# End of routing: gathers for nine chunks, hi and lo rows for the last two, two remainders on another engine

## The chip, the cores and the metric

The kernel runs on one core of a Trainium2 chip. The metric is the device time of one execution in microseconds. Before the change the median of three runs is 744.73 us (744.6 to 744.79). The time contains everything from the first load to the last write of the output.

## The reference

Retention, then a mixture of experts with capacity, then a dense mixture of four experts. Cut to what matters:

```python
# retention, B=2, H=8, S=768, head 64, x = y as (N=1536, D=512)
state = gamma * state + k_t (outer) v_t;  y_t = scale * q_t @ state
# first mixture: E=8, F=1024, capacity cap = N // E * 2 = 384
logits = x @ w_gate;  expert = argmax(logits);  gate = softmax(logits)[expert]
for i in range(N):            # in token order
    e = expert[i]
    if counts[e] < cap: disp[e, counts[e]] = x[i]; pos[i] = counts[e]; counts[e] += 1
y = relu(disp @ w1) @ w2;     out[i] = gate[i] * y[expert[i], pos[i]]
# second mixture: 4 experts on every token, weighted with normalised domain_probs
out += p[:, e] * (relu(x @ w1[e]) @ w2[e])
```

What the part below turns on: each token needs its expert, its rank among the tokens of that expert, and the rows of an expert must stand together before its matmuls can start.

## The kernel before

The 1536 tokens are 12 chunks of 128 (NT = 12). A first stage goes chunk by chunk through retention and routing, a second runs the eight experts of the first mixture on 224 slots each, a third the second mixture. Products in the second and third stage are three fp32r passes over high and low halves; `split_w` makes these halves for a block of weights: ScalarE casts the loaded block into the high half (line 124), and VectorE subtracts that from the block for the low half, the remainder (line 125).

The order of the work is written by hand: each engine runs its instructions in the order in which the program issues them. In the first stage, step `it` of the loop issues for chunk it-1 the state products, the state update, the second half of the output and its scaling (`st_I`, `st_U`, `st_O`, `st_x`), for chunk `it` the scores and their mask (`st_S`), for chunk it-2 the transposition with the gate logits (`x_pe`; `x_reduce` adds up the logits on VectorE, copies the rows to SBUF on ScalarE and writes them to `xd` in DRAM) and the argmax (`x_dve`), and for chunk it-3 the rank (`r_pe`, `r_dve`) with a slot matrix `at`, which says which token stands in which slot; `g_pe` turns it into indices in `slot_ps`. PSUM banks without a name of their own go round in fours, so that a tile needs the bank of the tile four before it.

Expert 0 is prepared apart, because it is needed first. For the chunks below NE = NT - 2 = 10, the indices of its slots are cast into `gidx0`, and GpSimd fetches its rows from `xd` with two indirect DMAs into `xe0`; `fetched` turns them with products against the identity into `xt0`. The rows of the last two chunks are added to `xt0` straight from SBUF: `r_dve` makes a one-hot matrix `at0` (which token of the chunk is in which slot of expert 0), and `late` multiplies the chunk's rows by it, as fp32.

At the end of routing the order is: state products of chunk 11, transposition of chunk 10, second half of chunk 11, index and gathers, transposition of chunk 11, one-hot products of chunk 10, of chunk 11, then the products on the gathered rows. `split_w(0)` stands in step 8 of the loop, `split_w(1)` behind all products. Then every engine reads a flag (line 580) and branches on it (line 581), ScalarE and VectorE split `xt0` into high and low halves (lines 713 and 717), and the matmuls of expert 0 begin (lines 860 and 863).

Weight blocks are loaded by SP into four buffers (`load_w`, line 111); a block's buffer is free when both its halves are made.

The lines quoted in words here are those of the profile:

Of the kernel before, what the change touches and what calls it, by code (L numbers as in the profile page):

```python
# [9 lines left out]
F32 = mybir.dt.float32  # L10
F32R = mybir.dt.float32r
F16 = mybir.dt.float16
I32 = mybir.dt.int32
AF = mybir.ActivationFunctionType
ALU = mybir.AluOpType
# [5 lines left out]
P = 128  # L21
B, H, S, HD = 2, 8, 768, 64
N, D, F = 1536, 512, 1024
E1, E2 = 8, 4
NCH = S // P
NT = N // P
NE = NT - 2
KD = D // P
KF = F // P
XW = KD * 136  # L30
# [25 lines left out]
def tile_retention_moe_moe(ctx: ExitStack, tc, qkv, cst, gqt, a1, a2, b1, b2, out, cap):  # L56
# [54 lines left out]
            nc.sync.dma_start(out=raws[u], in_=wsrc(u))  # L111
            nload[0] += 1

    def split_w(n):
        if n >= len(units) or units[n] in ws:
            return
        u = units[n]
        kind = u if isinstance(u, int) else u[0]
        if kind == "t":
            r = ts.pop(u[1])  # L120
        else:
            r = raws.pop(u)
        w = pw.tile([P, 2, 1024], F32R, tag="w", name=f"w{n}")
        nc.scalar.copy(w[:, 0], r)  # L124
        nc.vector.tensor_tensor(out=w[:, 1], in0=r, in1=w[:, 0].bitcast(F32), op=ALU.subtract)  # L125
        ws[u] = w
        if kind != "t":
            load_w(place[u] + 5)
# [47 lines left out]
    with ExitStack() as actx:  # L176
# [104 lines left out]
        def st_I(i):  # L281
            c = i % NCH
            live[i]["o"] = [bank(f"O{i}_{j}") for j in range(2)]
            q = live[i].pop("q")
            if c > 0:
                for hp in range(4):
                    for j in range(2):
                        r = slice(64 * j, 64 * j + 64)
                        nc.tensor.matmul(
                            out=o_at(i, hp, j), lhsT=st[c % 2][r, hp],  # L290
                            rhs=q[r, hp * P:(hp + 1) * P], start=(hp < 2), stop=False,
                            skip_group_check=True,
                        )
# [105 lines left out]
        def r_dve(i):  # L399
            rp = rl.pop(i)  # L400
            sel = p2.tile([P, 8], F32, tag="sel", name=f"sel{i}")
            rk = ranks[:, i:i + 1]
            yield nc.vector.tensor_tensor_reduce(
                out=sel, in0=rp, in1=ohs[:, i], scale=1.0, scalar=0.0, op0=ALU.mult, op1=ALU.add,
                accum_out=rk,
            )
            if i < NE:
                yield slot_at(i)
            else:
                at0[i] = p2.tile([P, SM], F32, tag="at0", name=f"at0_{i}")  # L410
                yield nc.vector.tensor_scalar(
                    out=at0[i], in0=rnk[:, 0:SM], scalar1=rk, scalar2=oh0.pop(i), op0=ALU.is_equal,
                    op1=ALU.mult,
                )

        def slot_at(i):
            at = ats[i] = p2.tile([P, SL], F16, tag="at", name=f"at{i}")
            return nc.vector.tensor_scalar(
                out=at, in0=rnk, scalar1=ranks[:, i:i + 1], scalar2=None, op0=ALU.is_equal
            )  # L420
# [16 lines left out]
        for it in range(NT):  # L437
# [27 lines left out]
                r_pe(it - 3)  # L465
                seqs.append(r_dve(it - 3))
            braid(*seqs)
            if it == 8:
                split_w(0)

        st_I(NT - 1)
        x_pe(NT - 2)
        r_pe(NT - 3)
        st_O(NT - 1)
        braid(r_dve(NT - 3))
        g_pe(NT - 4)
        g_pe(NT - 3)
        st_x(NT - 1)
        nc.vector.tensor_copy(gidx0, slot_ps[:, :, 0])
        xe0 = pq.tile([P, SL // P, D], F32, tag="kv", name="xe0")  # L480
        for b in range(SL // P):
            nc.gpsimd.indirect_dma_start(
                out=xe0[:, b], out_offset=None, in_=xd[0:1 + NE * P],
                in_offset=bass.IndirectOffsetOnAxis(ap=gidx0[:, b:b + 1], axis=0),
            )
        braid(x_dve(NT - 2))
        x_pe(NT - 1, False)
        r_pe(NT - 2)
        braid(r_dve(NT - 2))
        x_reduce(NT - 1)  # L490
        braid(x_dve(NT - 1))
        xt0 = [
            bank(f"T0x{g}", f"x{g}")[:, 0:2 * SM].rearrange("p (k t) -> p k t", k=2)
            for g in range(2)
        ]

        def late(i, ks=range(KD)):
            for k in ks:
                nc.tensor.matmul(
                    out=xt0[k // 2][:, k % 2], lhsT=xks[i][:, k * P:(k + 1) * P], rhs=at0[i],  # L500
                    start=(i == NE and k % 2 == 0), stop=True, skip_group_check=True,
                )

        def fetched(b, ks):
            w = min(SM - b * P, P)
# [4 lines left out]
                    start=False, stop=True, skip_group_check=True,  # L510
                )

        late(NE, range(KD - 1))
        r_pe(NT - 1)
        cps = bank("cnt")[:, 0:8]
        nc.tensor.matmul(out=cps, lhsT=onesb, rhs=cum[:, NT], start=True, stop=True)
        late(NE, range(KD - 1, KD))
        braid(r_dve(NT - 1))
        slot_at(NT - 2)
        slot_at(NT - 1)  # L520
        late(NE + 1)
        g_pe(NT - 2)
        g_pe(NT - 1)
        for ks in (range(2), range(2, KD)):
            fetched(0, ks)
            fetched(1, ks)
        nc.vector.tensor_scalar(
            out=cnt[:, 0], in0=cps, scalar1=float(cap), scalar2=None, op0=ALU.min
        )
# [1 line left out]
        if general:  # L531
# [7 lines left out]
                )  # L539
            nc.vector.tensor_copy(nbi[:, 0:8], nbf)  # L540
            nc.vector.tensor_reduce(out=nbi[:, 8:9], in_=nbf, axis=AX.X, op=ALU.max)
        split_w(1)
        nc.vector.tensor_copy(gidx, slot_ps)

    def offsets():
# [759 lines left out]
```

## Time and profile before

| | |
|---|---|
| median of three runs | 744.73 us |
| the profiled execution | 744.18 us |
| its span, first to last instruction | 742.4 us |
| TensorE busy | 727.5 us (98%) |
| VectorE, ScalarE, GpSimd busy | 469.0, 338.8, 167.6 us |
| first matmul of expert 0 | 68.13 us from the start of the span |
| mean granted TensorE clock | 0.997 |

A time in a row is microseconds from the span's start, the number behind it how long the piece took. A merged row of TensorE counts its pieces (x16); matmuls overlap, so a row's length is from its first start to its last end. An fp32 product shows as two instructions, an fp32r one as one. In brackets stands how long the engine was idle ahead of the row, and what ended that.

### The profile page before, as it was taken

Reading aid. Unit: us, or ns where it says so; the run is one execution under the profiler, and the core shown is the slowest. Engines: PE = TensorE matmul, PEld = TensorE weight load, DVE = VectorE, ACT = ScalarE, POOL = GpSimd, SP = SyncE. Lnnn points to the kernel's source line nnn. Section 1 sums busy time; section 2 is a strip of 40 time slices with the busy share of each in tenths; the row PEclk is TensorE's granted clock in tenths of the full one; section 3 lists DMA queues with packets and bytes.
Section 4 is the critical chain, followed back from the end, with each engine's and each line's share of the span. In section 5 each row is a group of like instructions: output and inputs, shape, how many; then the busy total and the mean of one; then the engine's idle time right before and its main releaser. Section 6 shows DMA issues by size and latency. Waiting matters only on the chain.

```text
span 742.4 us, 11359 instructions
## 1 busy us (share of the span) xinstructions
PE 727.5 (98%) x4466; PEld 661.8 (89%) x4467; DVE 469.0 (63%) x769; ACT 338.8 (46%) x545; POOL 167.6 (23%) x158
## 2 busy tenths in 40 slices
PE   8998999999999999999999999999999999999996
PEld 5887999999998888899988999889998899988895
DVE  4888889887887935634754645773375454557334
ACT  2334666675665624334443335633445334453341
POOL 3543111222310011222222211213421121111103
PEclk9999999999999999999999999999999999999998
DMA  9985876687561122211113122112221212112002
GB/s 336 409 325 160 298 259 217 214 277 240 201 200 57 40 75 64 103 61 57 57 60 100 41 85 86 58 62 95 100 72 72 86 56 86 58 57 86 29 0 86
DMA packets 27642, 93.22 MB, mean 126 GB/s; under 512 B 3617, under 2 KB 3889, under 8 KB 27586
## 3 DMA queue, kind: packets, MB, share of 16 engines
q1 hardware_dynamic: 23042, 81.79, 31.9%
q0 software_dynamic: 2672, 7.44, 3.2%
q10 hardware_dynamic: 1872, 3.24, 1.1%
q8 instruction: 36, 0.59, 0.3%
q14 instruction: 20, 0.16, 0.1%
HBM read 86.11 MB, written 6.34 MB: 125 GB/s over the span
## 4 chain that ended last, share of the span: by engine, by line
PE 85%; DVE 5%; DMA 5%; ACT 1%; issue 1%; POOL 1%; POOLq 0%; SPq 0%; ACTq 0%; DVEq 0%
PE o L1111 35%; PE a L955 17%; PE m L860 11%; PE b L955 8%; PE m L863 5%; PE bb L955 5%; DMA kv<-qkv 2%; DVE w L125 2%; DMA qk<-qkv 1%; DMA xd<-xk 1%; DVE tsum L889 1%; PE O L301 1%; PE S L246 1%; DMA raw<-a 1%; PE T L701 1%
## 5 line engine op out<-in xcount | busy, mean ns | idle before, releaser
L1111 PE MATMUL o<-w,g_c 128*128 128x512 f32 x1152 | 267.4, 390 | 0.0
L1111 PEld LDWEIGHTS o<-w,g_c 128*128 128x128 f32 x1152 | 215.8, 188 | 43.8
L125 DVE TENSOR_TENSOR w<-raw,w 128x1024 fp32r<-128x1024 f32 x128 | 158.2, 1245 | 16.9 <-ACT w L124 16.7
L955 PE MATMUL a<-X,w 128*128 128x384 f32 x720 | 145.1, 336 | 0.0
L124 ACT CAST w<-raw 128x1024 fp32r<-128x1024 f32 x128 | 132.6, 1048 | 5.9 <-DMA raw<-a 4.2
L990 DVE TENSOR_TENSOR c<-b,c 128x384 f32<-128x384 f32 x30 | 16.7, 558 | 181.2 <-PE b L955 181.2
L955 PEld LDWEIGHTS a<-X,w 128*128 128x128 f32 x720 | 127.3, 188 | 2.6 <-DVE c L990 0.3
L139 POOL TENSOR_TENSOR t<-raw 128x512 f32<-128x512 f32 x28 | 38.8, 1386 | 375.2 <-DMA raw<-b 326.9
L986 ACT COPY c<-a 128x384 f32<-128x384 f32 x60 | 28.7, 479 | 196.4 <-PE a L955 196.4
L860 PE MATMUL m<-h,w 128*128 128x448 f32 x256 | 81.7, 378 | 1.7 <-DVE h L890 1.7
L860 PE MATMUL m<-xet,w 128*128 128x448 f32 x256 | 80.8, 375 | 0.9 <-DVE xet L717 0.9
L971 ACT ACTIVATE g_c<-c 128x384 fp32r<-128x384 f32 x96 | 50.4, 526 | 66.2 <-DVE c L990 64.9
L955 PE MATMUL b<-X,w 128*128 128x384 f32 x360 | 72.0, 334 | 0.0
L863 PE MATMUL m<-h,w 128*128 128x224 f32 x256 | 67.4, 263 | 0.0
L863 PE MATMUL m<-xet,w 128*128 128x224 f32 x256 | 67.4, 263 | 0.0
L955 PEld LDWEIGHTS b<-X,w 128*128 128x128 f32 x360 | 63.5, 188 | 0.0
L975 DVE SCALAR_TENSOR_TENSOR g_c<-c,g_c 128x384 fp32r<-128x384 f32 x96 | 52.9, 552 | 4.0
L860 PEld LDWEIGHTS m<-h,w 128*128 128x128 f32 x256 | 48.0, 187 | 6.1 <-ACT w L124 2.2
L860 PEld LDWEIGHTS m<-xet,w 128*128 128x128 f32 x256 | 48.0, 187 | 4.7 <-PEq L581 1.0
L863 PEld LDWEIGHTS m<-h,w 128*128 128x128 f32 x256 | 48.8, 191 | 0.0
L863 PEld LDWEIGHTS m<-xet,w 128*128 128x128 f32 x256 | 48.8, 190 | 0.0
L955 PE MATMUL bb<-X,w 128*128 128x384 f32 x204 | 41.3, 339 | 0.1
(148 smaller groups left out, 747.1 us busy)
## 6 DMA issues: line engine op xcount, KB each, us to landing
raw<-a SPq DMA_DIRECT2D x64, 512.0 KB, 4.3
raw<-b SPq DMA_DIRECT2D x64, 512.0 KB, 3.5
qk<-qkv SPq DMA_DIRECT2D x12, 512.0 KB, 8.4
kv<-qkv SPq DMA_DIRECT2D x12, 512.0 KB, 8.3
xd<-xk ACTq DMA_DIRECT2D x12, 256.0 KB, 6.6
gqs<-gqt SPq DMA_DIRECT2D x6, 256.0 KB, 7.7
iw<-cst SPq DMA_DIRECT2D x1, 272.0 KB
xe<-xd,gidx POOLq DMA_INDIRECT x16, 4.2
```

What stands on the lines that cost most here:

```text
L124: nc.scalar.copy(w[:, 0], r)
L125: nc.vector.tensor_tensor(out=w[:, 1], in0=r, in1=w[:, 0].bitcast(F32), op=ALU.subtract)
L139: eng.tensor_tensor(out=c[:, 0:2], in0=b[:, 2:4], in1=b[:, 1:3], op=sub)
L246: nc.tensor.matmul(out=bks[j][:, cols], lhsT=qk[r, 1, cols], rhs=qk[r, 0, cols], start=True, stop=True,)
L860: nc.tensor.matmul(out=b2, lhsT=w[0], rhs=x, start=first, stop=last, skip_group_check=True)
L863: nc.tensor.matmul(out=b2[:, 0], lhsT=w[1], rhs=x[:, 0], start=False, stop=last, skip_group_check=True)
L955: nc.tensor.matmul(out=bk[:, 0:HT], lhsT=w[:, sw, k], rhs=x[:, sx, k], start=(first and m == 0), stop=(m == len(steps) - 1), skip_group_ch ...
L971: nc.scalar.activation(out=h2[:, 0], in_=src, func=AF.Relu)
L975: nc.vector.scalar_tensor_tensor(out=h2[:, 1], in0=src, scalar=0.0, in1=h2[:, 0].bitcast(F32), op0=ALU.max, op1=ALU.subtract,)
L986: nc.scalar.copy(t, bk[:, 0:HT])
L990: nc.vector.tensor_tensor(out=t, in0=bk[:, 0:HT], in1=t, op=ALU.add)
L1111: nc.tensor.matmul(out=bk, lhsT=h2[:, sh, cols], rhs=w[:, sw, k], start=(q == 0 and m == 0 and (n, t) not in begun), stop=(m == 2), skip_g ...
```

## The change

Four things move at the end of routing; what is computed stays the same.

- NE becomes NT - 3 = 9: the gathers cover nine chunks, and chunk 9 is added with one-hot products too, in fp32 as before.
- For chunks 10 and 11 the one-hot products are fp32r: `x_parts` casts the rows on ScalarE and takes the low rows on GpSimd, and `late` multiplies both by the one-hot matrix, high rows first.
- The output of chunk 11 is finished ahead of the transposition of chunk 10, and index and gathers come right after it. The products on gathered rows stand between those of chunk 10 and those of chunk 11.
- `split_w(0)` and `split_w(1)` go into steps 10 and 11 of the loop, with the subtraction on GpSimd.

```diff
-NE = NT - 2
+NE = NT - 3
-    def split_w(n):
+    def split_w(n, eng=nc.vector):
...
         nc.scalar.copy(w[:, 0], r)
-        nc.vector.tensor_tensor(out=w[:, 1], in0=r, in1=w[:, 0].bitcast(F32), op=ALU.subtract)
+        eng.tensor_tensor(out=w[:, 1], in0=r, in1=w[:, 0].bitcast(F32), op=ALU.subtract)
...
-                at0[i] = p2.tile([P, SM], F32, tag="at0", name=f"at0_{i}")
+                at0[i] = p2.tile([P, SM], F32R if i > NE else F32, tag="at0", name=f"at0_{i}")
...
-            at = ats[i] = p2.tile([P, SL], F16, tag="at", name=f"at{i}")
+            at = ats[i] = p2.tile([P, SL], F16, tag="at", name=f"at{i}", bufs=3)
...
-            if it == 8:
-                split_w(0)
-
-        st_I(NT - 1)
-        x_pe(NT - 2)
-        r_pe(NT - 3)
-        st_O(NT - 1)
-        braid(r_dve(NT - 3))
-        g_pe(NT - 4)
-        g_pe(NT - 3)
-        st_x(NT - 1)
-        nc.vector.tensor_copy(gidx0, slot_ps[:, :, 0])
...
-        braid(x_dve(NT - 2))
-        x_pe(NT - 1, False)
-        r_pe(NT - 2)
-        braid(r_dve(NT - 2))
-        x_reduce(NT - 1)
-        braid(x_dve(NT - 1))
...
+            if it >= NT - 2:
+                split_w(it - NT + 2, nc.gpsimd)
+
+        parts = {}
+
+        def x_parts(i):
+            x = parts[i] = pq.tile([P, 2, D], F32R, tag="qk", name=f"xs{i}")
+            nc.scalar.copy(x[:, 0], xks[i])
+            nc.gpsimd.tensor_tensor(
+                out=x[:, 1], in0=xks[i], in1=x[:, 0].bitcast(F32), op=ALU.subtract
+            )
+
+        def late(i, ks):
+            x = xks[i] if i == NE else parts[i]
+            for s in range(1 if i == NE else 2):
+                for k in ks:
+                    cols = slice(k * P, (k + 1) * P)
+                    nc.tensor.matmul(
+                        out=xt0[k // 2][:, k % 2], lhsT=x[:, cols] if i == NE else x[:, s, cols],
+                        rhs=at0[i], start=(i == NE and k % 2 == 0), stop=True,
+                        skip_group_check=True,
+                    )
...
-        late(NE, range(KD - 1))
-        r_pe(NT - 1)
-        cps = bank("cnt")[:, 0:8]
-        nc.tensor.matmul(out=cps, lhsT=onesb, rhs=cum[:, NT], start=True, stop=True)
-        late(NE, range(KD - 1, KD))
-        braid(r_dve(NT - 1))
-        slot_at(NT - 2)
-        slot_at(NT - 1)
-        late(NE + 1)
-        g_pe(NT - 2)
-        g_pe(NT - 1)
-        for ks in (range(2), range(2, KD)):
-            fetched(0, ks)
-            fetched(1, ks)
+        k01, k23 = range(2), range(2, KD)
+        st_I(NT - 1)
+        st_O(NT - 1)
+        st_x(NT - 1)
+        g_pe(NE - 1)
+        r_pe(NE)
+        nc.vector.tensor_copy(gidx0, slot_ps[:, :, 0])
...
+        x_pe(NT - 2, False)
+        braid(r_dve(NE))
+        x_reduce(NT - 2)
+        x_parts(NT - 2)
+        x_pe(NT - 1, False)
+        braid(x_dve(NT - 2))
...
+        late(NE, k01)
+        r_pe(NT - 2)
+        late(NE, k23)
+        x_reduce(NT - 1)
+        x_parts(NT - 1)
+        braid(r_dve(NT - 2), x_dve(NT - 1))
+        late(NT - 2, k01)
+        r_pe(NT - 1)
+        cps = bank("cnt")[:, 0:8]
+        nc.tensor.matmul(out=cps, lhsT=onesb, rhs=cum[:, NT], start=True, stop=True)
+        late(NT - 2, k23)
+        slot_at(NE)
+        slot_at(NT - 2)
+        braid(r_dve(NT - 1))
+        slot_at(NT - 1)
+        g_pe(NE)
+        fetched(0, k01)
+        fetched(1, k01)
+        g_pe(NT - 2)
+        late(NT - 1, k01)
+        g_pe(NT - 1)
+        fetched(0, k23)
+        fetched(1, k23)
+        late(NT - 1, k23)
...
-        split_w(1)
```

On GpSimd, before, from the scaled values of chunk 9 (`vg9`) on to the gathers of expert 0's rows and the flag:

```order
L230 TENSOR_TENSOR vg9_715<-kv9_573,cdec_109 128x512
L316 TENSOR_TENSOR xT8_800<-ot8_801,gqs_110 128x512
L230 TENSOR_TENSOR vg10_805<-kv10_649,cdec_109 128x512
L316 TENSOR_TENSOR xT9_877<-ot9_878,gqs_110 128x512
L230 TENSOR_TENSOR vg11_882<-kv11_732,cdec_109 128x512
L482 DMA xe0_1047<-xd_68,gidx0_77 128x512 x2
L580 TENSOR_LOAD nbi_92
```

The same place after it (`w0`, `w1` are remainders of weights, `xs10` and `xs11` low rows):

```order
L316 TENSOR_TENSOR xT9_872<-ot9_873,gqs_110 128x512
L230 TENSOR_TENSOR vg11_877<-kv11_732,cdec_109 128x512
L125 TENSOR_TENSOR w0_922<-raw0_575,w0_922 128x1024
L125 TENSOR_TENSOR w1_1002<-raw1_651,w1_1002 128x1024
L509 DMA xe0_1034<-xd_68,gidx0_77 128x512 x2
L476 TENSOR_TENSOR xs10_1055<-xk10_1037,xs10_1055 128x512
L476 TENSOR_TENSOR xs11_1090<-xk11_1058,xs11_1090 128x512
L599 TENSOR_LOAD nbi_92
```

Two subtractions of weights stand ahead of the gathers now, and two of rows behind them.

On TensorE, before, from the last rank (`R11`) to the flag; `T0x0` and `T0x1` are the halves of `xt0`:

```order
L329 MATMUL R11_1094<-cum_79,onesb_74 128x8
L330 LDWEIGHTS ub_73
L330 MATMUL R11_1094<-ohs_80,ub_73 128x8
L516 LDWEIGHTS onesb_74
L516 MATMUL cnt_1097<-cum_79,onesb_74 128x8
L499 MATMUL T0x1_1090<-at0_10_1072,xk10_1010 128x224
L499 MATMUL T0x0_1089<-at0_11_1102,xk11_1059 128x224 x2
L499 MATMUL T0x1_1090<-at0_11_1102,xk11_1059 128x224 x2
```

And after it, from chunk 10's products on the first half:

```order
L485 MATMUL T0x0_1075<-at0_10_1098,xs10_1055 128x224 x4
L329 LDWEIGHTS onesb_74
L329 MATMUL R11_1110<-cum_79,onesb_74 128x8
L330 LDWEIGHTS ub_73
L330 MATMUL R11_1110<-ohs_80,ub_73 128x8
L532 LDWEIGHTS onesb_74
L532 MATMUL cnt_1113<-cum_79,onesb_74 128x8
L485 MATMUL T0x1_1076<-at0_10_1098,xs10_1055 128x224 x4
```

The last rank and the counts stand behind four products that read chunk 10's high and low rows; before, they stood behind three products of chunk 10 that read its fp32 rows.

## Rows read from the trace of the kernel before

**Rows 1.** Busy time by stretch: start:end, length, each engine's busy us, clock, DMA.

```profile
250.00:740.00 490.00, 485.83 (x2432) 439.02 (x2430) 266.20 (x371) 198.72 (x314) 102.48 (x100) 1.00 0.20 69
```

**Rows 2.** Timeline of TensorE at the end of routing: start, length, what, idle before.

```profile
55.81 0.67 PE L289 MATMUL O<-qk,st 64*64 64x128 f32 x16
...
57.69 1.15 PE L301 MATMUL O<-sd,vg 128*64 128x128 f32 x16
...
59.37 1.19 PE L344 MATMUL X<-iw,xT 128*128 128x136 f32 x8 [0.35 <-DVE xT L320]
...
61.43 1.37 PE L499 MATMUL T0x<-at,xk 128*128 128x224 f32 x6 [0.83 <-DVE lgs L359]
...
63.54 1.78 PE L499 MATMUL T0x<-at,xk 128*128 128x224 f32 x8 [0.20 <-DVE at L411]
...
65.26 2.00 PE L507 MATMUL T0x<-ident,xe 128*128 128x128 f32 x16
68.13 0.44 PE L860 MATMUL m<-xet,w 128*128 128x448 f32 x1 [0.86 <-DVE xet L717]
68.41 0.27 PE L863 MATMUL m<-xet,w 128*128 128x224 f32 x1
68.51 0.37 PE L860 MATMUL m<-xet,w 128*128 128x448 f32 x1
```

**Rows 3.** Line 581, the branch, TensorE's sequencer: duration ns, first and last start.

```profile
L581 PEldq EVENT_SEMAPHORE  x2: 51/51/51, 67.3 to 67.5; - x2
```

**Rows 4.** Timeline of GpSimd: the gathers of expert 0's rows.

```profile
60.00 1.15 POOL L482 DMA_INDIRECT xe<-xd,gidx  x1 [7.74 <-DVE cd L376]
61.45 0.97 POOL L482 DMA_INDIRECT xe<-xd,gidx  x1 [0.30 <-issue]
```

**Rows 5.** Line 482, the gathers: us from issue to landing.

```profile
DMA to landing us min/median/max: 4.1/4.1/4.2
```

**Rows 6.** Timeline of VectorE: w0's remainder, last output, index cast, last one-hot matrix.

```profile
45.07 1.22 DVE L125 TENSOR_TENSOR w<-raw,w 128x1024 fp32r<-128x1024 f32 x1 [1.18 <-ACT w L124]
...
58.89 0.76 DVE L320 TENSOR_TENSOR xT<-O,gqs 128x256 f32<-128x256 f32 x2 [0.26 <-PE O L301]
59.56 0.15 DVE L479 CAST gidx<-slot_ps 128x2 int32<-128x2 f32 x1
...
63.09 0.40 DVE L411 TENSOR_SCALAR at<-kc,ranks,oh 128x224 f32<-128x224 f32 x1
```

**Rows 7.** Timeline of TensorE: state products of chunks 9 and 10.

```profile
46.42 1.19 PE L289 MATMUL O<-qk,st 64*64 64x128 f32 x16
...
51.38 0.67 PE L289 MATMUL O<-qk,st 64*64 64x128 f32 x16
```

**Rows 8.** Timeline of ScalarE: writes of chunks 8 and 9, and w1's cast.

```profile
52.35 0.33 ACTq L366 DMA_DIRECT2D xd<-xk  x1
...
56.79 0.33 ACTq L366 DMA_DIRECT2D xd<-xk  x1
...
62.49 1.04 ACT L124 CAST w<-raw 128x1024 fp32r<-128x1024 f32 x1 [0.40 <-ACT xk L363]
```

**Rows 9.** GpSimd by line and shape: count, busy us, mean ns, idle before.

```profile
L316 POOL TENSOR_TENSOR xT<-ot,gqs 128x512 f32<-128x512 f32 x10 | 12.9, 1289 | 10.2 <-ACT ot L315 8.2 <-issue 1.6 <-POOL vg L230 0.4
...
L767 POOL TENSOR_TENSOR s<-x 128x768 f32<-128x768 f32 x2 | 4.7, 2335 | 0.0
...
L767 POOL TENSOR_TENSOR s<-x,s 128x768 f32<-128x768 f32 x1 | 1.8, 1846 | 0.0
```

**Rows 10.** Busy time by stretch, columns as in rows 1: near the start, near the end.

```profile
6.00:7.60 1.60, 0.20 (x4) 0.01 (x1) 1.29 (x2) 0.00 (x0) 1.03 (x1) 1.00 1.04 419
...
737.60:737.80 0.20, 0.00 (x0) 0.00 (x0) 0.00 (x0) 0.00 (x0) 0.20 (x1) 0.99 1.04 430
737.80:738.00 0.20, 0.00 (x0) 0.00 (x0) 0.00 (x0) 0.00 (x0) 0.20 (x1) 0.50 1.04 430
```

**Rows 11.** Timeline of TensorE: the last products of the run.

```profile
727.69 8.13 PE L1111 MATMUL o<-w,g_c 128*128 128x512 f32 x35
```

More of the change, by code (lines that the diff above doesn't have):

```diff
@@ L467, in tile_retention_moe_moe @@
             braid(*seqs)
-            if it == 8:
-                split_w(0)
-        st_I(NT - 1)
-        x_pe(NT - 2)
-        r_pe(NT - 3)
-        st_O(NT - 1)
-        braid(r_dve(NT - 3))
-        g_pe(NT - 4)
-        g_pe(NT - 3)
-        st_x(NT - 1)
-        nc.vector.tensor_copy(gidx0, slot_ps[:, :, 0])
[L480 to L484, printed above, removed]
-            )
-        braid(x_dve(NT - 2))
-        x_pe(NT - 1, False)
-        r_pe(NT - 2)
-        braid(r_dve(NT - 2))
-        x_reduce(NT - 1)
-        braid(x_dve(NT - 1))
[L492 to L502, printed above, removed]
+            if it >= NT - 2:
[6 more added lines that the diff above has]
+                out=x[:, 1], in0=xks[i], in1=x[:, 0].bitcast(F32), op=ALU.subtract
+            )
+        def late(i, ks):
[8 more added lines that the diff above has]
+                    )
         def fetched(b, ks):
@@ L511, in fetched @@
                 )
-        late(NE, range(KD - 1))
+        k01, k23 = range(2), range(2, KD)
[5 more added lines that the diff above has]
+        nc.vector.tensor_copy(gidx0, slot_ps[:, :, 0])
+        xe0 = pq.tile([P, SL // P, D], F32, tag="kv", name="xe0")
+        for b in range(SL // P):
+            nc.gpsimd.indirect_dma_start(
+                out=xe0[:, b], out_offset=None, in_=xd[0:1 + NE * P],
+                in_offset=bass.IndirectOffsetOnAxis(ap=gidx0[:, b:b + 1], axis=0),
+            )
[5 more added lines that the diff above has]
+        braid(x_dve(NT - 2))
+        xt0 = [
+            bank(f"T0x{g}", f"x{g}")[:, 0:2 * SM].rearrange("p (k t) -> p k t", k=2)
+            for g in range(2)
+        ]
+        late(NE, k01)
[5 more added lines that the diff above has]
+        late(NT - 2, k01)
         r_pe(NT - 1)
```

## The prediction

> **What bounds the kernel now.** I read the busy shares by stretch first: from 250 to 740 us TensorE is busy 485.83 of 490 us [rows 1], so whatever happens before the expert stage is not made good there; the end of the run follows the first expert matmul one for one. In the kernel before that matmul starts at 68.13 [rows 2]. The whole question is how early it can start, and the reader should see in the order of time who holds it.
>
> On TensorE the last chunks of routing run from 55.81 to 67.26 [rows 2]: state products of chunk 11, then its second half (57.69), its transposition with the gate (59.37), the one-hot products of chunk 10 (61.43) and of chunk 11 (63.54), and the 16 instructions on gathered rows (65.26, 2.00). Idle before them is small: 0.35, 0.83, 0.20. After them come 0.87 us until 68.13: the branch on the overflow flag. Its event semaphore on TensorE's sequencer is at 67.3 [rows 3], when the last product has ended, so the jump begins only after TensorE has drained. The end of the last product plus 0.87 is the start of the experts.
>
> The gathers are hidden, but only just. GpSimd starts them at 60.00 and 61.45 [rows 4], they land 4.1 and 4.2 us later [rows 5], at 64.1 and 65.65; the first product on the second gather is the fifth of the 16 instructions from 65.26; they stand some 0.116 us apart (2.00 us less about 0.26 of the last one's tail, over 15), which makes 65.7.
>
> **The change part by part.**
>
> *First remainder leaves VectorE.* At 45.07 VectorE subtracts for w0 after 1.18 us idle for ScalarE's cast [rows 6], and the mask multiply of chunk 9 stands behind it. The next state products need the bank that this multiply reads: they take 1.19 us where the same 16 instructions take 0.67 a chunk later [rows 7]. TensorE is otherwise gapless there, so 0.52 us comes back: everything that follows moves to its time before minus 0.52, if nothing new is late. ScalarE's two casts (1.04 us each [rows 8]) now stand in chunks 10 and 11, behind the copies of chunks 8 and 9. The first runs from 52.35 + 0.33 + 0.04 - 0.52 = 52.2 to 53.25 and puts the state copy for chunk 11 behind it, to 53.6; TensorE asks for that at 55.29. The second is done before chunk 10's copies are due at 58.4. So nothing, and up to 1.04 each if that cover were gone. SP's fifth and sixth weight loads now wait for GpSimd's subtractions; behind them on SP stands nothing before the branch, and their weights are split only inside expert 0: nothing. The third buffer of the slot matrices costs nothing either.
>
> *Last output first.* O of chunk 11 no longer has the transposition of chunk 10 ahead of it. Its state products start at 55.81 - 0.52 = 55.29; 0.67 and 1.15 us, overlapping by some 0.1 [rows 2], let VectorE read at 57.0. It needs 0.67 to the index cast's start (58.89 to 59.56); the cast comes at 57.75 instead of 59.56 [rows 6]. Nine chunks suffice for it, the write of chunk 9 is no longer waited for. Taken alone this starts the gathers 1.8 us earlier.
>
> *Second remainder goes in front of them.* In GpSimd's order the w1 subtraction now stands right ahead of the gathers. It waits for ScalarE's cast, and that stands behind the copies of chunk 9 and their DMA issue: 56.79 + 0.33 + 0.04 - 0.52 = 56.64, cast 1.04 [rows 8], done 57.68. The subtraction of 128x1024 on GpSimd is not in the trace. Nearest rows: 128x512 in 1.289 us, 128x768 in 1.846 and, in another form, 2.335 [rows 9]. The first two give 2.18 ns per element, so 1.846 + 256 x 2.18 ns = 2.40 us. Lower bound 1.85 (no less than for 768), upper 4/3 of 2.335 = 3.11; I take 2.40, the line through the two nearest forms. It runs 57.73 to 60.13, and the gathers, ready at 57.9, start at 60.43 and 61.87 (0.30 between GpSimd pieces, 1.15 for the first [rows 4]), and land 4.1 to 4.2 later at 64.55 and 66.0. What was won on the index is lost here, and 0.35 more.
>
> *Hi and lo rows.* Two products' worth of fp32 becomes two fp32r passes. The fp32 form takes 1.78 us for four products in eight instructions, some 1.62 without the last one's tail; the 224-column form of the experts takes 0.10 to the next start (68.41 to 68.51 [rows 2]), so eight take 0.8 to 0.9. That removes about 1.5 us of TensorE in two chunks, against 1.62 that chunk 9 adds: no change of work. But the low rows come from GpSimd, behind both gathers: the second leaves GpSimd at 61.87 + 0.97 = 62.84, then 1.29 us [rows 9] per chunk: chunk 10 at 64.2, chunk 11 at 65.5. On TensorE the order is strict. X of 10 and 11 from 57.15 to 59.2, chunk 9's four products to 60.95, two high products at 61, then a wait for chunk 10's low rows until 64.2. Queued behind it are the rank matmul of chunk 11, the counts, and through VectorE the last one-hot matrix: it comes near 65.3 (before, 63.09 plus 0.40 [rows 6]), still ahead of the second gather.
>
> *The tail.* Products of chunk 10 to 65.0, first gather to 65.5, then the second gather at 66.0 ends last. Behind it: 4 instructions 0.46, slot 0.05, four chunk-11 products 0.44, slot 0.05, eight on gathered rows 0.92, four products 0.44: 68.36, and the last one ends 0.15 later, 68.51. Plus 0.87 is 69.38. Against 68.13 that is +1.25 us; with the bounds of the subtraction +0.7 to +1.95. ScalarE and VectorE finish the high and low halves of the first two blocks by 68.5, inside that. The extra load that the w1 subtraction releases (512 KB, 1.25 us at the 419 GB/s of a full stretch [rows 10]) falls on the first gather, which has half a microsecond to spare; I take nothing, at most 1.25 for the range. The Trainium skill, DMA: Bandwidth & Descriptors, section Issuing engines are not separate DMA queues, says that transfers started by different engines interleave on the same 16 DMA engines; by it the sum would carry up to those 1.25.
>
> *Clock.* The wait from 61.2 to 64.2 is the first long one with TensorE idle since the start. At the end of the run the last products run from 727.69 for 8.13 us, to 735.82 [rows 11]; the granted clock is 0.99 over 737.60 to 737.80 and 0.50 right after [rows 10]: it fell to the 1.2 GHz level 2.0 us after TensorE, busy until then, went idle. In 6.00 to 7.60, with 0.20 of 1.60 busy, it stood at 1.00 [rows 10]. Three microseconds, with two short products in them, are nearer to the first. The work after the wait is 3.5 us of products at 2.4 GHz; at 1.2 GHz it takes up to 3.5 more, but about 1 us of waits for the gather absorbs some and the clock can rise before the end: +0.6 to +1.8, I take +1.1. The Trainium skill, TensorE: Matmul & The Clock Gate, section What's actually happening, says that the low level is the default and that recent activity releases it. By that rule the time is the sum with the clock term; the rows above bear it out once at the end of the run.
>
> **Against the measured time.** The profiled run took 744.18 for a span of 742.4; the median of the runs is 744.73, 0.55 above it. Differences are put on the median. A measurement of this kernel can tell about 0.2%, 1.49 us, from no change: under 743.24 is faster, over 746.22 slower.
>
> **The rivals.**
>
> *Forecast, clock falls:* +1.25 + 1.1 = +2.35, 747.1 (746.3 to 748.5). For it: the order on GpSimd, and the fall 2.0 us after the last product at the end. Against: the two high products inside the wait, and the 1.4 us of idle near the start that left it.
>
> *Same delay, clock holds:* +1.25, 746.0, which counts as no change; with the bounds 745.4 to 746.7. For it: only one fall is seen in the whole run. Both cases decide on the one wait for chunk 10's low rows.
>
> *The subtraction does not hold the gathers (the other side):* if it costs GpSimd little, the gathers start at 57.9 + 0.3 = 58.2 and 59.65 and land at 62.35 and 63.8; the low rows are there at 62.0 and 63.3, the wait falls to one microsecond, and the same tail of 2.51 + 0.87 after 63.8 starts the experts at 67.2, 0.95 before now: 743.8. It decides from a subtraction of 1.2 us, at which the sum is zero (60.43 becomes 59.2, all behind it 1.2 earlier). Against it: 1.289 us for half as many elements. For it: GpSimd's spans are rough, and the form is not in the trace.
>
> *More on the gathers:* the load in front of them or a slower subtraction on top of the clock: 748.5 to 749.5.
>
> **How the numbers follow.** Clock falls 45%, clock holds 25%, gathers not held 25% (a fifth of that under 743.24, where TensorE's work ends even earlier than in my tail), more on the gathers 5%. Slower: nearly all of the first, a third of the second, the last: 0.44 + 0.09 + 0.05 = 0.58. Faster 0.05, the rest 0.37. The range 744.0 to 748.5 leaves out most of the last case and the better half of the third.
>
> **What would show it.** In the profile after: the state products of chunk 9 at 0.67 and not 1.19; GpSimd's 128x1024 row near 2.4 and the first gather near 60.4 right behind it; a TensorE wait of 3 us for GpSimd's low rows; the granted clock at 0.50 or 1.00 from 64 to 68; the first expert matmul at 69.4 with the clock held, 70.5 without. It is wrong if the gathers start near 58.2, or if the second one lands later than 66.5, or if a wait in the expert stage takes up the delay.

## The result, and the profile after

The changed kernel takes 750.81 us (median of six runs, 749.1 to 752.29) where the kernel before, on the same chip, takes 744.76: ratio 1.0079, 95% interval 1.0062 to 1.0096, so 0.8% slower. The profiled execution took 749.56 for a span of 747.8; before it was 744.18 for 742.4. So the span grew by 5.4 us.

Three points of the timeline divide it. From the start to the state products of chunk 11 the changed kernel is 0.37 us shorter (55.44 instead of 55.81, [rows 2]). From there to the first expert matmul it takes 17.28 us instead of 12.32; I call this piece the stretch, and every experiment is measured by it. After the first expert matmul (72.72 instead of 68.13) it takes 0.81 longer. -0.37 + 4.96 + 0.81 = 5.40.

First the state products of chunks 9 and 10 (timeline of TensorE: start, length, engine, line, what, count), which answer [rows 7]:

```profile
46.57 0.67 PE L289 MATMUL O<-qk,st 64*64 64x128 f32 x16
51.01 0.67 PE L289 MATMUL O<-qk,st 64*64 64x128 f32 x16
```

Both take 0.67; the 0.52 us of chunk 9 is gone. Then the timeline of VectorE, GpSimd and TensorE from w0's subtraction to the first expert matmul, in order of start (in brackets: idle before, and what ended it), which answers [rows 2, 4, 6]:

```profile
53.48 2.36 POOL L125 TENSOR_TENSOR w<-raw,w 128x1024 fp32r<-128x1024 f32 x1 [1.59 <-ACT w L124]
...
54.34 1.29 DVE L251 TENSOR_TENSOR sd<-S,cdec 128x512 f32<-128x512 f32 x2 [0.31 <-PE S L246]
...
57.24 0.76 DVE L320 TENSOR_TENSOR xT<-O,gqs 128x256 f32<-128x256 f32 x2
57.91 0.15 DVE L506 CAST gidx<-slot_ps 128x2 int32<-128x2 f32 x1
57.91 2.34 POOL L125 TENSOR_TENSOR w<-raw,w 128x1024 fp32r<-128x1024 f32 x1 [2.07 <-ACT w L124]
57.98 0.15 DVE L403 CUSTOM_DVE_ANT_0 sel<-R,ohs 128x8 f32<-128x8 f32 x1
...
58.18 2.21 DVE L411 TENSOR_SCALAR at<-kc,ranks,oh 128x224 f32<-128x224 f32 x1
...
60.42 1.15 POOL L509 DMA_INDIRECT xe<-xd,gidx  x1 [0.17 <-DVE at L411]
...
60.80 0.23 DVE L376 SCALAR_TENSOR_TENSOR cd<-lgs,mxs,kc 128x8 f32<-128x8 f32 x1
...
60.93 1.02 PE L485 MATMUL T0x<-at,xk 128*128 128x224 f32 x4 [1.60 <-ACT xk L363]
...
61.87 0.97 POOL L509 DMA_INDIRECT xe<-xd,gidx  x1 [0.30 <-issue]
...
62.27 3.10 DVE L376 SCALAR_TENSOR_TENSOR cd<-lgs,mxs,kc 128x8 f32<-128x8 f32 x1
...
62.85 2.50 POOL L476 TENSOR_TENSOR xs<-xk,xs 128x512 fp32r<-128x512 f32 x2
...
65.30 0.39 DVE L411 TENSOR_SCALAR at<-kc,ranks,oh 128x224 fp32r<-128x224 f32 x1
...
65.83 0.68 PE L485 MATMUL T0x<-at,xs 128*128 128x224 f32 x4 [2.99 <-DVE cm L379]
...
67.33 2.00 PE L494 MATMUL T0x<-ident,xe 128*128 128x128 f32 x8
...
71.12 0.68 PE L485 MATMUL T0x<-at,xs 128*128 128x224 f32 x4
...
72.72 0.44 PE L879 MATMUL m<-xet,w 128*128 128x448 f32 x1 [0.91 <-DVE xet L736]
```

Read it by comparing each row with its twin, the same instruction elsewhere. One small VectorE instruction, L376 on 128x8, takes 0.23 us for chunk 10 and 3.10 for chunk 11. L411 takes 0.40 in the kernel before [rows 6] and 2.21 here for chunk 9. Both long rows end within 0.14 us of a GpSimd instruction's end: w1's subtraction (57.91 + 2.34 = 60.25; VectorE 60.39) and the second low-row subtraction (62.85 + 2.50 = 65.35; VectorE 65.37). Not every VectorE row beside GpSimd is long: L251, which reads PSUM, takes its usual 1.29 for two in the middle of w0's subtraction (53.48 to 55.84), and L506 and L403, which read PSUM too, take 0.15 beside the start of w1's.

On TensorE, I call the products on the high and low rows of chunks 10 and 11 the hi/lo products. The row at 65.83 holds the first four of chunk 10, two on high rows and two on low rows. They waited for VectorE: they need the one-hot matrix of chunk 10 (L411, 65.30 to 65.69), and in VectorE's order this stands right behind L376 of chunk 11. The low rows were there before, at 64.14.

The 0.68 and 1.02 of TensorE's products in fp32r and fp32 are as expected; the 2.00 for eight instructions at 67.33 is not: [rows 2] have 16 in that time. The granted clock says why (start:end, length, busy us of the five engines, clock, DMA share, GB/s):

```profile
66.00:66.60 0.60, 0.60 (x8) 0.58 (x8) 0.60 (x6) 0.00 (x0) 0.00 (x0) 1.00 0.40 154
66.70:70.00 3.30, 3.30 (x20) 3.22 (x19) 1.64 (x11) 0.00 (x0) 0.00 (x0) 0.50 0.00 0
70.10:72.00 1.90, 1.71 (x16) 1.49 (x15) 0.23 (x2) 0.69 (x2) 0.00 (x0) 1.00 0.03 9
```

After TensorE's 2.99 us of idle time the clock is at its 1.2 GHz level from 66.7 to 70.0, while TensorE is busy throughout. The gathers' landing, which answers [rows 5]:

```profile
DMA to landing us min/median/max: 4.9/5.0/5.1
```

### The profile page after: what moved, and what is told of

It reads as the page before. It is cut to its first block, busy times and chain, and to the rows that moved or that the text cites. A ratio compares the mean times of both kernels' runs of the same rounds, so it can differ in the third digit from the quotient of the medians.

```text
span 747.8 us, 11383 instructions
## 1 busy us (share of the span) xinstructions
PE 729.5 (98%) x4474; PEld 663.2 (89%) x4475; DVE 470.5 (63%) x769; ACT 340.3 (46%) x547; POOL 171.1 (23%) x162
## 4 chain that ended last, share of the span: by engine, by line
PE 82%; DVE 4%; issue 1%; DMA 1%; ACT 1%; POOL 1%; POOLq 0%; DVEq 0%; ACTq 0%
PE o L1130 34%; PE a L974 17%; PE m L879 11%; PE b L974 8%; PE m L882 5%; PE bb L974 5%; DVE w L125 1%; DVE tsum L908 1%; DMA raw<-a 1%; PE T L720 1%; POOL out_dram L1142 1%; DMA raw<-b 1%; PE ab L974 0%; DVE h L909 0%; DVE x L786 0%
## 5 line engine op out<-in xcount | busy, mean ns | idle before, releaser
L125 DVE TENSOR_TENSOR w<-raw,w 128x1024 fp32r<-128x1024 f32 x126 | 155.4, 1243 | 16.4 <-ACT w L124 16.1
```

The source lines that it names most:

```text
L125: eng.tensor_tensor(out=w[:, 1], in0=r, in1=w[:, 0].bitcast(F32), op=ALU.subtract)
```

## The experiments

Fifteen kernels ran (one is the changed kernel again), each beside the kernel before on the same chip, where that takes 744.96 to 745.40 in the median. Theories: **1, hold**: a VectorE instruction that reads and writes SBUF stands still while a GpSimd tensor instruction runs. **2, queue**: only GpSimd's order counts. **3, data**: the long VectorE rows wait for something that GpSimd's last instruction releases. **Clock**, and **load**: the weight loads that the early subtractions release slow the gathers and writes beside them.

| kernel | stretch, us | median | ratio to before (95%) |
|---|---|---|---|
| before | 12.32 | 744.76 | |
| changed | 17.28 | 750.81 | 1.0079 (1.0062 to 1.0096) |
| changed, again | 18.33 | 750.34 | 1.0066 (1.0045 to 1.0088) |
| w1 on VectorE | 13.88 | 748.48 | 1.0048 (1.0033 to 1.0063) |
| low rows on VectorE | 14.79 | 750.22 | 1.0071 (1.0047 to 1.0094) |
| both on VectorE | 15.05 | 746.75 | 1.0028 (1.0007 to 1.0049) |
| GpSimd in pieces | 17.05 | 750.74 | 1.0076 (1.0060 to 1.0093) |
| changed + filler | 15.69 | 749.67 | 1.0062 (1.0043 to 1.0081) |
| both on VectorE + filler | 13.29 | 746.31 | 1.0023 (1.0009 to 1.0037) |
| fp32 products | 13.83 | 748.95 | 1.0050 (1.0034 to 1.0067) |
| before, w0 moved | 13.97 | 746.19 | 1.0010 (1.0000 to 1.0019) |
| before, w0 moved, load late | 14.17 | 745.82 | 1.0013 (1.0002 to 1.0023) |
| both on VectorE, load late | 16.61 | 750.00 | 1.0062 (1.0048 to 1.0077) |
| changed, loads late | 18.31 | 750.92 | 1.0070 (1.0056 to 1.0085) |
| before, w1 on GpSimd | 13.44 | 746.25 | 1.0006 (0.9997 to 1.0016) |
| order only | 15.65 | 748.30 | 1.0038 (1.0026 to 1.0049) |
| hold, load, clock away | 13.17 | 746.50 | 1.0020 (1.0008 to 1.0032) |

A stretch is of one profiled execution, so it holds that execution's clock. The clock fell inside the stretch in seven of these profiles: the changed kernel, the same again, both on VectorE, GpSimd in pieces, the two of the new order with loads late, and order only.

### Is the hold real, and what does it cost?

**w1 back on VectorE.**

```diff
-            if it >= NT - 2:
-                split_w(it - NT + 2, nc.gpsimd)
+            if it == NT - 2:
+                split_w(0, nc.gpsimd)
...
+        split_w(1)
         nc.vector.tensor_copy(gidx, slot_ps)
```

> The changed kernel with the w1 remainder back on VectorE at the end of routing, nothing else. Both theories: the slot matrix of chunk 9 (L411, 58.18 to 60.39 in the changed kernel, 2.21 us) takes 0.40 again and the gathers start near 58.2 and 59.65. Theory 1 (a VectorE instruction on SBUF operands does not end while a GpSimd tensor instruction runs): the two low-row subtractions, now from about 60.6 to 63.2, still hold a VectorE instruction of chunk 10 or 11 until about 63.2, the first expert matmul comes at 68.9 to 70.5, the time is 745.5 to 747.5. Theory 2 (only GpSimd's order matters: w1 ahead of the gathers, low rows behind them): low rows at 62.0 and 63.3, no long VectorE row, first expert matmul 67.2, time 743.8.

Its timeline of VectorE, GpSimd and TensorE:

```profile
58.83 0.40 DVE L411 TENSOR_SCALAR at<-kc,ranks,oh 128x224 f32<-128x224 f32 x1
59.00 1.24 POOL L509 DMA_INDIRECT xe<-xd,gidx  x1 [2.51 <-DVE ranks L403]
...
61.06 3.01 DVE L376 SCALAR_TENSOR_TENSOR cd<-lgs,mxs,kc 128x8 f32<-128x8 f32 x1
...
61.52 2.51 POOL L476 TENSOR_TENSOR xs<-xk,xs 128x512 fp32r<-128x512 f32 x2
...
69.97 0.45 PE L880 MATMUL m<-xet,w 128*128 128x448 f32 x1 [1.08 <-DVE xet L737]
```

L411 is back at 0.40 and the first gather at 59.00: this execution's stretch begins 0.65 us later (56.09), and 58.2 plus 0.65 is 58.85. L376 moves with the low rows and ends with them (64.07, GpSimd 64.03). The long row stayed, as theory 1 wants; theory 2 had none. The stretch, 13.88, is in the range that I gave; the median, 748.48, is 1 us over it.

**The same work in pieces**: the four subtractions each cut into four instructions.

```diff
-        eng.tensor_tensor(out=w[:, 1], in0=r, in1=w[:, 0].bitcast(F32), op=ALU.subtract)
+        step = 1024 if eng is nc.vector else 256
+        for a in range(0, 1024, step):
+            eng.tensor_tensor(
+                out=w[:, 1, a:a + step], in0=r[:, a:a + step],
+                in1=w[:, 0, a:a + step].bitcast(F32), op=ALU.subtract,
+            )
...
```

> The changed kernel with GpSimd's subtractions cut into four instructions each (w0 and w1 in columns of 256, low rows in columns of 128); same work, same engine, same order. Theory 1: VectorE goes on when the piece that runs ends: the slot matrix of chunk 9 takes 0.4 to 1.0 instead of 2.21 and the choice of chunk 11 (L376) under 1.0 instead of 3.10, later instructions being held for a piece each; first expert matmul 1.5 to 3 us earlier than 72.72. Theory 3 (the two VectorE rows are waits for data or a buffer that GpSimd's last instruction releases): both rows stay at 2.2 and 3.1 or longer, time 750 to 752.

```profile
58.42 2.82 POOL L127 TENSOR_TENSOR w<-raw,w 128x256 fp32r<-128x256 f32 x4 [1.64 <-ACT w L124]
...
58.86 0.42 DVE L416 TENSOR_SCALAR at<-kc,ranks,oh 128x224 f32<-128x224 f32 x1
...
59.93 0.64 DVE L381 SCALAR_TENSOR_TENSOR cd<-lgs,mxs,kc 128x8 f32<-128x8 f32 x1
...
62.00 0.23 DVE L381 SCALAR_TENSOR_TENSOR cd<-lgs,mxs,kc 128x8 f32<-128x8 f32 x1
...
62.77 0.45 PE L492 MATMUL T0x<-at,xs 128*128 128x224 f32 x2 [0.43 <-DVE cm L384]
...
64.36 1.02 PE L492 MATMUL T0x<-at,xs 128*128 128x224 f32 x2 [1.14 <-POOL xs L482]
```

The slot matrix of chunk 9 (now L416) takes 0.42 in the middle of a subtraction that goes on for 2 us more. That rules out theory 3: nothing that the last piece releases was waited for. The choice of chunk 11 (now L381, at 62.00) proves less, because the low rows' pieces begin only at 63.83. The end of the hold shows on TensorE too: the first hi/lo product starts 6.82 us behind the state products of chunk 11 (55.95) instead of 10.39. No time came back, though: the pieces take 2.82 instead of 2.34 and, for the low rows, 3.51 instead of 2.50, so that TensorE now waits 1.14 for the low rows; the clock is at 0.50 from 65 to 71, and the first expert matmul comes at 73.00. The rows were forecast rightly, the gain of 1.5 to 3 us was not there.

**One hold put into the kernel before**: its w1 subtraction on GpSimd, behind the gathers.

```diff
         x_reduce(NT - 1)
+        split_w(1, nc.gpsimd)
...
-        split_w(1)
```

> The kernel before with only w1's remainder moved, from VectorE's last place (64.75, 1.22 us) to GpSimd, behind its gathers and behind ScalarE's cast, so 63.6 to 66.0. VectorE builds the slot matrices of chunks 10 and 11 at 63.4 to 64.0 there. Theory 1: the second of them (0.31 us alone) lasts until 66.0, the instructions on gathered rows wait for it, and the first expert matmul comes 0.8 us later than in the kernel before: 746.1 beside 745.3. Theory 3 (no hold, only waits for data): VectorE saves 1.22 us, nothing waits, 745.3 or less.

```profile
64.00 2.71 DVE L418 TENSOR_SCALAR at<-kc,ranks 128x256 f16<-128x256 f32 x2
64.14 1.78 PE L500 MATMUL T0x<-at,xk 128*128 128x224 f32 x8 [0.20 <-DVE at L411]
64.22 2.35 POOL L125 TENSOR_TENSOR w<-raw,w 128x1024 fp32r<-128x1024 f32 x1 [1.19 <-ACT w L124]
...
66.77 0.20 PE L425 MATMUL slot_ps<-ohk,at 128*128 128x8 f16 x2 [0.82 <-DVE at L418]
```

The pair of slot matrices takes 2.71 instead of 0.61 and ends with GpSimd (66.71 and 66.57); TensorE waits 0.82 for it. The hold appears in the other kernel too, on another instruction. The stretch grows by 1.12. The ratio of the times, 1.0006, does not tell that from nothing.

**Low rows on VectorE, and both.** In the first only the low-row subtractions change engine (`nc.gpsimd` to `nc.vector`, issued behind the next chunk's choice); the second adds the edit of w1 above.

> The changed kernel with both low-row subtractions on VectorE (behind the six small instructions of each chunk's choice), w1 left on GpSimd ahead of the gathers. Theory 1: the slot matrix of chunk 9 still takes 2.2 us, until w1's subtraction ends near 60.3; the choice of chunk 11 (L376, 3.10 us in the changed kernel) takes 0.23; gathers at 60.4 and 61.9 as before; first expert matmul 69.4, clock held at 1.00 through 62 to 69, time 746.0. Theory 2: the low rows come off GpSimd's queue, gathers unchanged, and the time falls by what the wait for the low rows cost, 1 us at most: 749.

> The changed kernel with the w1 remainder and both low-row subtractions on VectorE, so that GpSimd runs only w0's subtraction and the gathers in this stretch. Theory 1: no VectorE row over 0.8 us between 57 and 65, gathers at 58.2 and 59.65, TensorE's waits under 1.5 us, clock at 1.00 throughout, first expert matmul 67.2, time 743.8 and the same in every run to 0.3. Theory 2: VectorE gets 1.24 us more in its chain and GpSimd's gathers come early: 744.5 to 745.

With the low rows alone on VectorE, L411 of chunk 9 is still at 2.21 and L376 of chunk 11 at 0.23, the clock holds 1.00 from 60 to 72, all as theory 1 wants; the stretch is 14.79, 0.8 more than the expected 69.4 gives, since VectorE's choice of chunk 11 now stands behind the low rows of chunk 10. The time, 4 us over my forecast, has another part: in the profiled execution the clock fell later, inside the experts:

```profile
230.00:235.00 5.00, 3.34 (x13) 2.94 (x14) 2.47 (x3) 1.91 (x3) 0.00 (x0) 0.76 0.23 89
```

With both on VectorE no VectorE row between 57 and 65 exceeds 0.8 us, as theory 1 said, and the time is 1.6 us over the kernel before, not under it: the clock fell again, after short waits of 1.13, 0.44 and 0.69 us, and the runs lie between 745.32 and 751.73.

```profile
66.00:68.00 2.00, 2.00 (x15) 1.93 (x16) 1.55 (x5) 0.53 (x1) 0.00 (x0) 0.69 0.00 0
68.00:70.00 2.00, 2.00 (x11) 1.96 (x10) 0.63 (x1) 0.00 (x0) 0.00 (x0) 0.50 0.70 258
```

### What does the clock cost?

Matmuls on zeros into an unused bank fill TensorE's waits: 12 ahead of the first hi/lo product in the changed kernel; 5 there and 3 ahead of the second gather's products in the kernel with both on VectorE. (`hold` in the diff is this filler, not theory 1.)

```diff
+        hold(12)
         late(NT - 2, k01)
```

> The changed kernel plus 12 matmuls of 128x128 by 128x512 on zeros into an unused bank, put on TensorE ahead of the first product on low rows, where it waited 2.99 us (62.84 to 65.83); 12 x 0.213 = 2.56 us, so they delay nothing. If the clock's fall is caused by that wait, the clock stays at 1.00 through 66 to 72, the time from the first product on low rows to the first expert matmul falls from 6.89 us to 5.44 (as with the clock held after the same wait when w1 is on VectorE), all runs lie within 0.7 us of each other, at 748 to 748.5. If the clock falls for another reason: 749 to 752.5 as in the changed kernel, with the same spread. The VectorE rows stay at 2.21 and 3.10 in both.

> The changed kernel with w1 and the low rows on VectorE, and matmuls on zeros in TensorE's two remaining waits (5 ahead of the first low-row product, 3 ahead of the second gather's). If the clock is what spread its runs from 745.3 to 751.7: all runs within 0.7 us, at 745.3 to 745.8. If the spread has another cause it stays at 6 us and the median near 746.8.

The changed kernel with filler, by stretches:

```profile
62.00:66.00 4.00, 3.81 (x20) 1.96 (x18) 3.97 (x10) 1.71 (x4) 3.48 (x3) 1.00 0.89 301
66.00:72.00 6.00, 4.87 (x44) 4.65 (x45) 4.14 (x24) 1.90 (x3) 0.43 (x1) 1.00 0.14 54
```

The clock stays at 1.00 and the stretch falls from 17.28 to 15.69, while the two long VectorE rows stay (2.22 and 3.12): the fall cost 1.59 us there, half of the 3.4 us that it lasted. The wait alone does not decide the fall, however. With w1 on VectorE TensorE waited 2.84 us at the same place, without filler, and the clock stayed:

```profile
62.00:64.00 2.00, 0.00 (x0) 0.00 (x0) 2.00 (x2) 1.51 (x2) 2.00 (x2) 1.00 0.85 286
64.00:66.00 2.00, 1.48 (x15) 1.46 (x16) 1.93 (x13) 0.00 (x0) 0.04 (x1) 1.00 0.48 179
```

The runs with filler did not come together as I expected (748.08 to 750.96, and 745.01 to 750.47 in the second kernel). The mean granted clock of the first four hardly differs (0.998 to 0.996), so a part of the spread has a cause that these runs don't show. **The changed kernel run again** shows the part that is the clock's; its median, 750.34, is just under the 750.5 to 751.5 that I gave:

> The changed kernel once more, beside the other kernels of the experiments. Median 750.5 to 751.5 (750.81 before), with the rows of 2.21 and 3.10 us on VectorE and a fall of the clock after TensorE's wait.

```profile
67.00:68.00 1.00, 1.00 (x8) 1.00 (x7) 0.93 (x6) 0.00 (x0) 0.00 (x0) 0.50 0.05 18
68.00:72.00 4.00, 4.00 (x22) 3.92 (x22) 0.86 (x5) 0.53 (x1) 0.00 (x0) 0.50 0.01 4
...
75.00:76.00 1.00, 1.00 (x5) 0.91 (x5) 1.00 (x2) 0.31 (x1) 0.92 (x1) 0.50 0.55 119
76.00:78.00 2.00, 2.00 (x11) 1.89 (x10) 1.48 (x2) 0.00 (x0) 1.47 (x2) 0.71 0.78 250
```

Here the same wait was followed by some ten microseconds at the low level, into the first expert, and this execution took 752.40 instead of 749.56. The same program loses 1.6 us or about three more, by when the clock comes back; what decides that, the rows do not show. Of the six runs in the result, the three at 751.67 to 752.29 have a mean granted clock of 0.991 to 0.993, the three at 749.1 to 749.95 one of 0.995 or 0.996.

### What do the loads cost?

**Only w0's remainder moved, in the kernel before** (the prediction's first step alone), and **the same with the released load issued late** by ScalarE (last line; in the first kernel SyncE issues it at 56.4):

```diff
-            if it == 8:
-                split_w(0)
+            if it == NT - 2:
+                split_w(0, nc.gpsimd)
...
         x_reduce(NT - 1)
+        HELD[0] = 0
+        load_w(5, nc.scalar)
...
```

> The kernel before with only w0's remainder moved: from VectorE in step 8 to GpSimd in step 10. Its 2.36 us on GpSimd (53.5 to 55.8) lie beside VectorE instructions that read PSUM, which ran at their usual length beside it in the changed kernel. By the prediction's first step the state products of chunk 9 take 0.67 instead of 1.19 and the end comes 0.5 us earlier: 744.6 beside 745.15. If the next chunk's wait takes it back: no difference.

> The kernel before with w0's remainder on GpSimd in step 10 (as in the run with w0 alone, where the gathers started at 62.08 because chunk 9's write landed 4.3 us after its issue instead of 2.8), and the weight load that this subtraction releases issued by ScalarE behind the last chunk's copies, near 62.5, instead of by SyncE at 56.4. Load theory (the 512 KB load beside the write and the gathers is what cost): the write lands in 2.8 us again, the gathers start within 0.3 of 4.2 us after the state products of chunk 11 as in the kernel before and land in 4.2, the state products of chunk 9 take 0.67, time 0.5 us under the kernel before. Otherwise: the gathers are late as in the run with w0 alone, time 0.9 over the kernel before.

In the first kernel the gathers start late, behind chunk 9's write (timeline of GpSimd; then the window 54 to 66 of the DMA issues: KB each, median us to landing):

```profile
62.08 1.15 POOL L482 DMA_INDIRECT xe<-xd,gidx  x1 [5.72 <-DVE cd L376]
```

```profile
xd<-xk ACTq DMA_DIRECT2D x3, 256.0 KB, 4.3
raw<-a SPq DMA_DIRECT2D x1, 512.0 KB, 4.1
```

The writes land in 4.3 us, 2.8 in the kernel before. The 0.52 us is won, and the end still comes 0.9 us later (746.19 beside 745.31). With the load at 62.12 the gathers start at 59.59, 4.19 behind the state products as before, so the load was the cause; but now it runs beside the gathers, the second lands after 6.0 us, and TensorE waits 1.58 for it. Half of the load theory held, and no time was won.

**The same two moves in kernels of the new order**:

> The changed kernel with w1 and the low rows on VectorE and the load that w0's subtraction releases issued by ScalarE near 63. Load theory: both gathers land 4.1 to 4.2 us after their issue (4.5 and 5.4 with the load), TensorE's 0.69 us wait for the second is gone, 745.5 median. Otherwise landing near 5.0 and 746.7 as without the edit.

> The changed kernel with only its two weight loads (issued at 55.87 and 60.28) held back to ScalarE near 64. Load theory for the rows: gathers land in 4.2 instead of 5.0 us, the writes of chunks 9 to 11 in 2.8 instead of 4.4. For the time: by theory 1 the VectorE rows of 2.21 and 3.10 us end last, not the gathers, so 749.5 to 751.5 as the changed kernel. If the loads are the larger cost: 747 or less.

In the changed kernel with both loads late the gathers land in 4.1 instead of 5.0 and the writes in 2.3 instead of 4.4, and the first hi/lo product still waits until 65.72, 2.99 us: the loads are not what holds the changed kernel. With both on VectorE the late load hit the second gather (6.2 us, a wait of 1.49), and the clock fell: worse, not better.

### What does the order cost by itself?

**fp32 products** (no hi and lo rows, w1 on VectorE), and **order only** (w0 back in step 8 as well):

> The changed kernel with w1 on VectorE and without hi and lo rows: the products of the last three chunks in fp32 straight from the copied rows, nothing of theirs on GpSimd or ScalarE. Theory 1 (GpSimd's instructions are what cost): no wait for low rows, about 1.6 us more of products on TensorE, first gather product waits for the landing; the first expert matmul comes 11.5 to 12.3 us after the state products of chunk 11 (17.28 in the changed kernel, 12.32 in the kernel before), time 744.3 to 745.2. Theory 2 (nine gathered chunks and three late ones make more work at the end): 13.5 us or more, 746.5.

> Only the order of the changed kernel: gathers for nine chunks, the last output first, fp32 products of three chunks, with both remainders on VectorE in their old places (step 8 and the end) and nothing else on GpSimd. No load runs beside the gathers, so they land in 4.2 us (5.1 with w0 on GpSimd), the wait of 1.29 us for the second is gone, and the first expert matmul comes 12.5 to 12.7 us after the state products of chunk 11: within 0.4 us of the kernel before, 745.3 to 745.8. If the third late chunk's products (2 us) are not covered by the earlier gathers: 746.5 or more.

> The changed kernel with hold, load and clock fall taken away: both remainders on VectorE in their old places, low rows on VectorE, five matmuls on zeros in TensorE's one wait. If these three are all there is, first expert matmul 12.4 to 12.8 us after the state products of chunk 11, gathers landing in 4.2, no wait over 1.3 us, 745.3 to 745.8. If something else of the 6 us is left: 746.5 or more.

Both fp32 kernels wait for the second gather, 1.29 and 1.69 us; in the second, with no load beside it until 65.9, it still took 5.3 us to land (66.2) and the first 4.1, and the clock fell behind that wait (0.50 from 68 to 70), which is in its 15.65. My expectations, 11.5 to 12.3 for the first and 12.5 to 12.7 for the second, were wrong. Why the second gather takes longer in this order, these runs don't show (the writes of chunks 10 and 11 run beside it). Without that wait the first has 12.54 us, where the kernel before, without its three waits [rows 2], has 10.94: the third chunk of fp32 products is 1.6 us more work.

The last kernel takes hold, load and clock fall away together: 13.17, over the 12.4 to 12.8 that I expected if these were all, and 0.85 over the kernel before; ratio 1.0020. So about 0.85 us is left for the order and the hi/lo products themselves: TensorE's wait ahead of the first of them (filled with 1.24 us of zeros), 0.44 for VectorE's slot matrix and 0.31 for the second gather, 1.99 together, are 0.61 more than the kernel before waits. No version is faster than the kernel before.

## Why the prediction was wrong

The forecast was 747.1, at most 748.5; it is 750.81. The direction was right, and so were the steps up to the gathers; the step on TensorE's wait ahead of the hi/lo products was not.

- **First remainder leaves VectorE**: right, 0.67 at both places and the stretch begins 0.37 earlier in the profiled execution (in all profiles with w0 moved it begins at 55.32 to 56.09, with w0 in step 8 at 55.81 to 56.42). That the load it releases costs nothing was wrong: the load slows the writes, and in the kernel before with w0 moved this starts the gathers 2 us late. In the changed kernel it did not decide.
- **Last output first**: right, cast forecast at 57.75, found at 57.91.
- **Second remainder in front of the gathers**: right, 2.34 for the 2.40 taken, gathers at 60.42 and 61.87 for 60.43 and 61.87. They land in 5.0, not 4.1, and in 4.1 again with the loads held back. The Trainium skill's rule that transfers started by different engines interleave on the same 16 DMA engines (DMA: Bandwidth & Descriptors, section Issuing engines are not separate DMA queues), on which I put a price of up to 1.25, agrees with the trace. The second gather so lands behind 66.7, which the prediction named as a sign of being wrong (later than 66.5), but nothing waits for it here.
- **Hi and lo rows: the step that failed.** The low rows of chunk 10 were forecast at 64.2 and ready at 64.14. But the forecast has TensorE on chunk 10's high rows at 61, and so takes its one-hot matrix as made by then; it came only at 65.69, because VectorE stood behind the subtractions, and TensorE started on high and low rows together at 65.83. I had costed GpSimd's instructions on GpSimd and on those who wait for their results, and VectorE's at their usual length. With the clock held the stretch is 15.69; the forecast has 69.38 - 55.29 = 14.09. Of the missing 1.60 us, 1.51 lie ahead of TensorE's start on the low rows: 10.42 us from the state products of chunk 11 (55.81 to 66.23), where the forecast has 8.91.
- **Clock**: it fell at the place forecast, and its price was inside the bounds: +1.1 taken (0.6 to 1.8), 1.59 measured against the filler. That it fell was in part luck: the wait of 2.84 us with w1 on VectorE left it at 1.00. That it can stay low into the experts, and cost some three more, was not in the range.
- **The rivals**: the forecast case came true with one term missing. "Gathers not held" fell with the 2.34 us row.

The 3.7 us between 747.1 and the median divide so: 2.09 in the stretch (1.51 the late one-hot matrix, 0.49 the clock, 0.09 the rest), 0.15 ahead of it, 0.81 behind it, and about 0.7 because the median lies 1.25 above the profiled execution, not 0.55 as before.

In the order of the runs, from the changed kernel's stretch of 17.28: clock held 15.69 (1.59), w1 off GpSimd 13.88 (1.81), low rows off GpSimd and waits filled 13.29 (0.59), w0 back in step 8 13.17 (0.12), against 12.32. Each is one execution, so the small steps are uncertain. The 0.81 us behind the first expert matmul I can't place: over the profiles that piece lies between 674.2 and 677.2.

The hold could have been read before. Timeline of the kernel before, VectorE's L367 on 128x8, which takes 0.17 when alone, beside GpSimd:

```profile
47.39 1.04 POOL L230 TENSOR_TENSOR vg<-kv,cdec 128x512 f32<-128x512 f32 x1
...
47.69 0.76 DVE L367 CUSTOM_DVE_ANT_0 lgs<-lgs,part 128x8 f32<-128x8 f32 x1
```

It ends at 48.45, GpSimd at 48.43. The Trainium skill says it too, and I did not weigh it: SBUF — State Buffer, section SBUF: two separate sides, has one pair of ports shared by VectorE and GpSimd, given whole to the instruction that starts first, against VectorE instructions in a two-port mode or, where GpSimd reads SBUF, with two SBUF inputs. Most rows above agree: L376 and L367 have two SBUF inputs, and the PSUM readers were not held. That L411 and L418, with one tensor input, use such a mode is not shown by a row, only that they are held; and L376 of chunk 11 starts ahead of GpSimd's row and is held all the same.

## What to carry to other kernels

Moving an elementwise instruction to GpSimd has a price on VectorE: ask which SBUF-only VectorE instructions fall into its time, and count each as lasting until GpSimd's instruction ends; the cheap place is beside VectorE's PSUM readers, as w0's was. Look for the sign of it in the trace of before: the same small instruction with two lengths. And an instruction that releases a buffer starts a load at that moment: check which write or gather will run beside it.

## What the runs showed of the hardware

- A VectorE instruction on 128x8 lasted 3.10 us instead of 0.23, to the end of two GpSimd subtractions on 128x512; one on 128x224 lasted 2.21 instead of 0.40, beside a subtraction on 128x1024. Cut into pieces, that subtraction let it through in 0.42.
- L376 of chunk 11 was held from 62.27, 0.58 us before GpSimd's row begins, and beside the second gather. The gather alone does not hold it: the same line took 0.23 beside the first gather, and in order only, without low rows, 0.23 beside the second (61.40, gather 60.87 to 61.83). Where GpSimd's subtraction really began, its row does not show.
- The same wait of 3.0 us was followed by 3.4 us at the 1.2 GHz level in one execution and some ten in another; a wait of 2.84 us in another kernel left the clock at 1.00.
